# Float64 weights in six staging places, the shifted words in PSUM, token weights in three pieces

## The chip, the cores and the metric

One core of a Trainium2 chip runs the whole program. The metric is the device time in microseconds (us). The kernel before takes 572.88 us, the median of three runs (572.08 to 574.86).

## The reference, cut to what matters

Four sequences (B = 4) of 576 tokens and 512 channels pass three layers:

```python
x = attn(q, k, v)                        # 8 heads of 64; 4 with a local mask, 4 with a strided one
theta = x @ w_theta                      # layer 2
yr = einsum('ts,bsd->btd', w_tok_r, x * cos(theta))
yi = einsum('ts,bsd->btd', w_tok_i, x * sin(theta))
u = x + yr + yi
x = u + maximum(u @ w_ch, 0)
out = moe2(x)                            # layer 3: 4 causal attention experts, top 2 of 4 by a gate
```

The weights `w_theta`, `w_tok_r`, `w_tok_i` and `w_ch` arrive as float64. The kernel turns each element into float32 and then into a pair hi + lo, because a product is computed as three matmuls: hi times hi, hi times lo, lo times hi.

## The kernel before, in words

X[b] (128 partitions, 4 chunks of 128 channels, 576 tokens) holds the activations of sequence b. The work runs in this order of text: layer 1 of sequence 0 (`attn_pair`, four pairs of heads of three groups each, in PSUM pool `ps0`), and between its pairs the loading of `wth`; then for each sequence b `theta` (two halves h of the channels, five tiles of tokens), `sines`, `rotate` (a TensorE transpose of X[b] into the PSUM tile `xn`, a VectorE product with cos and sin, the split into z_hi on ScalarE or VectorE and z_lo on GpSimd), `tokens` (y, nine chunks of three matmuls per output tile) and, one sequence later, `channels`. Layer 1 of sequence b + 1 is woven in by `next_pair`. Layer 3 follows for all sequences. A planner arranges the instructions of each engine's queue from this text and sets the waits. Each queue runs in order.

A float64 weight is loaded by `load64` in chunks. For each chunk SyncE issues a DMA of the raw pairs of words into X[3] (L127), ScalarE makes a float32 from the upper words with a scaled Prelu (L129, into a staging place `st` in X[2]), VectorE shifts and masks it in place (L130), and VectorE ors in the top bits of the lower words, in place again (L131). `split_w` then makes hi on ScalarE (L98) and lo on VectorE (L102 for the scaled `wth`, L100 where c % 3 == 1) or GpSimd (other L100). X[2] and X[3] are free at that time, since layer 1 has not yet reached sequences 2 and 3. Four chunks can be staged at a time. A new DMA waits until L131 has read the place that it overwrites. `wth` takes 8 chunks of 256 columns, `wtk` 18 of 288 (nine before the sines of half 0, nine behind them) and `wch` 8 of 256, 34 in all.

In PSUM each of eight banks holds 512 float32 per partition. `ps0` has four banks for scores, two for transposes and two for the values `av`; `ps1` has two for scores, one for transposes, two for `av`, one for `xn` and two for the accumulators of theta, y and g.

The sines of a half stand behind the last L129 of the `wtk` load before them on ScalarE (`behind`), and the second half of `wtk` stands behind the sines of half 0. `split_act` makes x_hi (L248) and x_lo (L250, GpSimd but for part of the first sequence of layer 3).

Of the kernel before, what the change touches and what calls it, by code (L numbers as in the profile page):

```python
# [24 lines left out]
HALF = S // 2  # L25
# [18 lines left out]
def fused_kernel(ctx: ExitStack, tc: tile.TileContext, ql, kl, vl, qs, ks, vs, wth, wtk, wch, wqk, wvg, wo, out):  # L44
# [71 lines left out]
    def load64(dst, src, kt, n0, n1, scale=1.0):  # L116

        hi, lo = dst
        n = n1 - n0
        for c in range(kt):
            raw = X[3].bitcast(U32)[:, c % 4, :2 * n].rearrange("p (n t) -> p n t", t=2)
            st = X[2][:, c % 4, :n]
            nc.sync.dma_start(raw, src[:, c, n0:n1].bitcast(U32).rearrange("p (n t) -> p n t", t=2))  # L127
            up, low, w = raw[:, :, 1], raw[:, :, 0], st.bitcast(U32)
            got = nc.scalar.activation(st, f(up), AF.Prelu, scale=2.0 ** -112, alpha=2.0 ** 32)  # L129
            nc.vector.tensor_scalar(w, w, 3, 0xFFFFFFF8, op0=ALU.logical_shift_left, op1=ALU.bitwise_and)  # L130
            nc.vector.scalar_tensor_tensor(w, low, 29, w, op0=ALU.logical_shift_right, op1=ALU.bitwise_or)  # L131
            split_w(hi[:, c, n0:n1], lo[:, c, n0:n1], st, scale, nc.vector if c % 3 == 1 else nc.gpsimd)
        return got.ins

    def per_tile(b, pair, g):

        return b == 0 and pair != 2 or b == 1 and g == 0

    ps_of, loaded = {}, {}
# [20 lines left out]
    def attn_pair(b, pair, ps1, apl, deep):  # L160
        ps_of[b] = ps1
# [59 lines left out]
    def values(b, pair, part, xo, turned):  # L221
# [3 lines left out]
        av = ps_of[b].tile([128, 512], F32, tag="av", bufs=2, name=f"av_{b}_{pair}_{r0}")  # L225
# [16 lines left out]
    def split_act(x, name):  # L242
        hi = act.tile([128, S], F32R, tag="ahi", name=f"{name}_hi")
        lo = act.tile([128, S], F32R, tag="alo", name=f"{name}_lo")
        if len(xsplit) == B:
            nc.scalar.copy(hi, x)
        else:
            nc.vector.tensor_copy(hi, x)  # L248
        eng = nc.vector if len(xsplit) == B and name.endswith(("0", "2")) else nc.gpsimd
        eng.tensor_tensor(lo, x, f(hi), op=ALU.subtract)  # L250
        return hi, lo
# [42 lines left out]
    def rotate(b, h):  # L294
        for t in range(NT):
            w, t0, cs = TW[t], 128 * t, trig[h, t]
            xn = ps1.tile([128, 512], F32, tag="xn", bufs=1, name=f"xn_{b}_{h}_{t}")
# [28 lines left out]
    def tokens(b, h):  # L326
        for n in range(2):
            sl = slice(HALF * n, HALF * (n + 1))
            for m in (2 * h, 2 * h + 1):
                c0 = 128 * (m % 2)  # L330
                y = ps1.tile([128, 512], F32, tag="acc", bufs=2, name=f"y_{b}_{m}_{n}")
                for c in range(9):
                    hi, lo = z[h, c]
                    mm3(y[:, :HALF], hi[:, c0:c0 + 128], lo[:, c0:c0 + 128], wtk_hi[:, c, sl], wtk_lo[:, c, sl],
                        c == 0, c == 8)
                u = X[b][:, m, sl]
                nc.vector.tensor_tensor(u, y[:, :HALF], u, op=ALU.add)  # L337
        for n in range(2):
            sl = slice(HALF * n, HALF * (n + 1))
# [28 lines left out]
    with tc.tile_pool(name="ps0", bufs=2, space=PSUM) as ps0, tc.tile_pool(name="ain0", bufs=9) as ain0, \  # L368
            tc.tile_pool(name="apl0", bufs=5) as apl0:
        for pair in range(4):  # L370
            load_pair(0, pair, ain0, 4, 4)
        attn_pair(0, 0, ps0, apl0, 2)
        attn_pair(0, 1, ps0, apl0, 2)
        for n0 in range(0, DM, 256):
            load64(wth_s, wth, 4, n0, n0 + 256, INV2PI)
# [5 lines left out]
    ps1 = ph1.enter_context(tc.tile_pool(name="ps1", bufs=2, space=PSUM))  # L381
    ain = pha.enter_context(tc.tile_pool(name="ain", bufs=3, side="right"))
# [8 lines left out]
    for b in range(B):  # L391
# [4 lines left out]
        else:  # L396
            sines(b, 0, angles, load64(wtk_s, wtk, 9, 0, HALF))
# [7 lines left out]
        else:  # L405
            with tc.issue_after(sins[0, 0]):
                ready = load64(wtk_s, wtk, 9, HALF, S)
# [15 lines left out]
        if b == 0:  # L423
            with tc.issue_after(sins[0, 1]):
                for n0 in range(0, DM, 256):
                    load64(wch_s, wch, 4, n0, n0 + 256)
# [332 lines left out]
```

## Time and profile before

| | |
|---|---|
| median of three runs | 572.88 us |
| profiled execution | 571.9 us, its span 570.1 us |
| TensorE busy | 533.8 us, 94% |
| VectorE busy | 407.2 us, 71% |
| ScalarE busy | 320.3 us, 56% |
| GpSimd busy | 231.1 us, 41% |
| mean granted TensorE clock | 0.97 |

The busy shares are means over stages of a different kind. The first 106 us (layer 1 of sequence 0, all loading of float64 weights, the first thetas and tokens) look different from the rest, and the change touches little outside them; so the profile is read by stretches of time. A row of a stretch gives the busy time of each engine with the count of instructions, then the granted clock, where 1.00 is 2.4 GHz and 0.50 is 1.2 GHz.

### The profile page before, as it was taken

The page shows a single profiled execution, that of the slowest core. Times are in us where ns is not written, and L with a number is a line of the kernel's source. Part 1 is how long each engine was busy: PE and PEld are TensorE (multiplying, and loading weights), DVE is VectorE, ACT ScalarE, POOL GpSimd, SP SyncE. Part 2 cuts the span into 40 slices and gives each one's busy share as a digit, 9 for nine tenths or more (in the row PEclk, how much of TensorE's full clock was granted, in tenths as well). Part 3 has the DMA queues.
Part 4 walks back from the last instruction along what each step waited for, and adds up shares of the span by engine and source line. Part 5 has one row for each costly group of instructions (what it writes and reads, how often), then busy time and mean ns, then how long its engine had stood idle before and what let it go on. Part 6 is the DMA issues. An engine that isn't in the chain of part 4 may idle for free.

```text
span 570.1 us, 12472 instructions
## 1 busy us (share of the span) xinstructions
PE 533.8 (94%) x4504; PEld 508.3 (89%) x4504; DVE 407.2 (71%) x1205; ACT 320.3 (56%) x904; POOL 231.1 (41%) x317
## 2 busy tenths in 40 slices
PE   7859698899999999999999999898999999999986
PEld 6749598899999999999999999897989999999986
DVE  3898889757686556766256553589988898888971
ACT  5875976525435326263152550376778668867873
POOL 3444566421156111545004570354455533634441
PEclk9959689999999999999999999999999999999998
DMA  9659443323122003110100020100001000100012
GB/s 299 208 171 317 126 153 96 97 86 131 31 86 86 23 17 132 37 30 1 56 1 1 1 58 0 39 1 2 0 12 43 33 1 32 54 1 12 33 43 85
DMA packets 19814, 37.55 MB, mean 66 GB/s; under 512 B 2328, under 2 KB 9672, under 8 KB 19752
## 3 DMA queue, kind: packets, MB, share of 16 engines
q1 hardware_dynamic: 19752, 36.74, 20.1%
q8 instruction: 36, 0.59, 0.5%
q14 instruction: 26, 0.21, 0.1%
HBM read 32.01 MB, written 4.72 MB: 64 GB/s over the span
## 4 chain that ended last, share of the span: by engine, by line
PE 60%; DVE 20%; ACT 11%; issue 3%; DMA 3%; POOL 1%; SPq 0%; DVEq 0%; POOLq 0%; ACTq 0%
PE y L254 6%; PE y L255 6%; PE y L256 6%; PE s L179 4%; DVE nm L588 3%; PE th L254 3%; DVE X L131 3%; PE th L256 3%; PE th L255 3%; PE g L255 2%; PE g L254 2%; PE g L256 2%; PE av L232 2%; ACT p L599 2%; PE tp L609 2%
## 5 line engine op out<-in xcount | busy, mean ns | idle before, releaser
L254 PE MATMUL y<-wtk_hi,zhi 128*128 128x288 f32 x288 | 86.5, 301 | 0.5 <-DVE X L337 0.4
L255 PE MATMUL y<-wtk_lo,zhi 128*128 128x288 f32 x288 | 85.9, 299 | 0.0
L256 PE MATMUL y<-wtk_hi,zlo 128*128 128x288 f32 x288 | 84.7, 296 | 0.0
L322 POOL TENSOR_TENSOR zlo<-cs,zhi 128x512 fp32r<-128x512 f32 (+1 forms) x40 | 48.4, 1222 | 66.5 <-DVE zhi L319 45.5
L206 POOL TENSOR_TENSOR p<-p,sm 128x288 f32<-128x288 f32 (+2 forms) x48 | 30.6, 644 | 92.7 <-DVE sm L205 49.0
L606 POOL TENSOR_SCALAR p<-p,sm,gt 128x256 f32<-128x256 f32 (+1 forms) x64 | 45.5, 714 | 51.9 <-DVE sm L604 35.5
L599 ACT ACTIVATE p<-s,nm 128x128 f32<-128x128 f32 (+2 forms) x96 | 49.6, 518 | 15.1 <-DVE nm L588 7.9
L254 PEld LDWEIGHTS y<-wtk_hi,zhi 128*128 128x128 f32 x288 | 54.0, 188 | 1.7 <-DVE X L337 1.1
L250 POOL TENSOR_TENSOR x_lo<-X,x_hi 128x576 fp32r<-128x576 f32 x24 | 35.7, 1492 | 46.9 <-DVE x_hi L248 40.6
L255 PEld LDWEIGHTS y<-wtk_lo,zhi 128*128 128x128 f32 x288 | 54.1, 188 | 0.3
L256 PEld LDWEIGHTS y<-wtk_hi,zlo 128*128 128x128 f32 x288 | 53.9, 188 | 0.1
L254 PE MATMUL th<-wth_hi,x_hi 128*128 128x256 f32 (+1 forms) x160 | 48.5, 303 | 3.3 <-ACT X L239 2.9
L588 DVE TENSOR_REDUCE nm<-s 128x1 f32<-128x128 f32 (+2 forms) x96 | 44.2, 468 | 5.3 <-PE s L586 4.4
L256 PE MATMUL th<-wth_hi,x_lo 128*128 128x256 f32 (+1 forms) x160 | 46.2, 290 | 0.0
L255 PE MATMUL th<-wth_lo,x_hi 128*128 128x256 f32 (+1 forms) x160 | 46.2, 289 | 0.0
L179 PE MATMUL s<-k,q 128*108 128x54 f32 (+2 forms) x320 | 44.0, 283 | 1.7 <-DMA k<-in_kl 1.7
L179 PEld LDWEIGHTS s<-k,q 128*108 128x108 f32 (+1 forms) x320 | 42.1, 204 | 2.7 <-DMA q<-in_ql 1.4
L213 ACT COPY pt<-tp 96x384 f32<-96x384 f32 (+2 forms) x44 | 20.9, 478 | 36.3 <-PE tp L209 36.1
L254 PE MATMUL pq<-x_hi,wqk_hi 128*128 128x288 f32 x128 | 39.8, 311 | 1.0 <-DVE q L534 0.9
L254 PE MATMUL g<-u_hi,wch_hi 128*128 128x288 f32 x128 | 39.2, 306 | 0.0
L618 DVE TENSOR_TENSOR ptlo<-tp,pthi 128x128 fp32r<-128x128 f32 (+4 forms) x80 | 37.6, 478 | 1.2 <-ACT pthi L617 0.6
L255 PE MATMUL pq<-x_lo,wqk_hi 128*128 128x288 f32 x128 | 38.0, 297 | 0.0
(170 smaller groups left out, 1716.3 us busy)
## 6 DMA issues: line engine op xcount, KB each, us to landing
X<-in_wtk SPq DMA_DIRECT2D x18, 288.0 KB
q<-in_qs SPq DMA_DIRECT2D x8, 594.0 KB
q<-in_ql SPq DMA_DIRECT2D x8, 576.0 KB
v<-in_vl SPq DMA_DIRECT2D x24, 144.0 KB
out_t<-X SPq DMA_DIRECT2D x16, 160.0 KB
k<-in_kl SPq DMA_DIRECT2D x8, 304.0 KB
k<-in_ks SPq DMA_DIRECT2D x8, 288.0 KB
X<-in_wth SPq DMA_DIRECT2D x8, 256.0 KB
```

What stands on the lines that cost most here:

```text
L179: nc.tensor.matmul(s[:rm, i * kw:i * kw + w], qt[:, j0 + i, :], kt[:, k0:k0 + w], start=False, stop=i == n - 1)
L206: nc.gpsimd.tensor_tensor(tiles(p), tiles(p), each(sm), op=ALU.mult)
L213: copy(pt[:kw, :n * rm], tp[:kw, :n * rm])
L250: eng.tensor_tensor(lo, x, f(hi), op=ALU.subtract)
L254: nc.tensor.matmul(ps, ahi, bhi, start=first, stop=False)
L255: nc.tensor.matmul(ps, ahi, blo, start=False, stop=False)
L256: nc.tensor.matmul(ps, alo, bhi, start=False, stop=last)
L322: nc.gpsimd.tensor_tensor(lo, zf, f(hi), op=ALU.subtract)
L588: nc.vector.tensor_reduce(nm[:w, t + ci:t + ci + 1], s[:w, :c1 - c0], axis=AX.X, op=ALU.max, negate=True)
L599: nc.scalar.activation(p[:w, c0:c1], scs[ci][:w, :c1 - c0], AF.Exp, bias=nm[:w, t:t + 1], scale=1.0, accum_out=acc)
L606: eng.tensor_scalar(p[:w, :kn], p[:w, :kn], sm[:w, t:t + 1], gt[:w, t, e:e + 1], op0=ALU.mult, op1=ALU.mult)
L618: nc.vector.tensor_tensor(dst(ptlo), src, f(dst(pthi)), op=ALU.subtract)
```

## The change

`load64` gets six staging places of 768 columns, three each in X[2] and X[3]; a place holds 512 words of raw pairs and 256 of `st`. They are used in turn over all loads, so a DMA waits for the chunk six before it. L130 no longer writes in place: it writes the shifted words to a piece `cv` of PSUM, and L131 reads the lower words from SBUF and `cv` from PSUM and writes `st`.

The PSUM for it is found by halving two banks. In `ps0` the two `av` tiles of sequence 0 become halves of one bank, and `cv` gets the two halves of the bank that is free. In `ps1` the `xn` tile becomes one persistent bank `xn_cv`: columns 0 to 255 take the transposes of `rotate`, 256 to 511 are `cv`.

A place holds 256 columns, so `wtk` is loaded in pieces of 256, 160 and 160 tokens, 27 chunks in place of 18. The first piece stands where the first half stood, the other two where the second half stood. `tokens` computes y in 256 and 320 tokens (`QCUT`) in place of 288 and 288, and splits u likewise; `channels` keeps 288 and 288.

Two smaller edits: all four x_lo of the first theta go to VectorE (`not xsplit` holds while the first list is built), and group 1 of the two local pairs of sequence 0 takes the softmax with one exponential for the group and VectorE's subtraction and sum, in place of one exponential with its own sum for each tile (`per_tile`).

```diff
--- before.py
+++ after.py
@@ -113,7 +113,7 @@
     def new_split(pool, kt, n, name):
         return tuple(pool.tile([128, kt, n], F32R, name=f"{name}_{part}") for part in ("hi", "lo"))
-    def load64(dst, src, kt, n0, n1, scale=1.0):
+    def load64(dst, src, kt, n0, n1, cvs, scale=1.0):
@@ -122,21 +122,26 @@
         hi, lo = dst
         n = n1 - n0
         for c in range(kt):
-            raw = X[3].bitcast(U32)[:, c % 4, :2 * n].rearrange("p (n t) -> p n t", t=2)
-            st = X[2][:, c % 4, :n]
+            at = len(staged) % 6
+            staged.append(n0)
+            place = X[2 + at // 3].rearrange("p c s -> p (c s)")[:, 768 * (at % 3):768 * (at % 3) + 768]
+            raw = place[:, :2 * n].bitcast(U32).rearrange("p (n t) -> p n t", t=2)
+            st = place[:, 512:512 + n]
             nc.sync.dma_start(raw, src[:, c, n0:n1].bitcast(U32).rearrange("p (n t) -> p n t", t=2))
             up, low, w = raw[:, :, 1], raw[:, :, 0], st.bitcast(U32)
             got = nc.scalar.activation(st, f(up), AF.Prelu, scale=2.0 ** -112, alpha=2.0 ** 32)
-            nc.vector.tensor_scalar(w, w, 3, 0xFFFFFFF8, op0=ALU.logical_shift_left, op1=ALU.bitwise_and)
-            nc.vector.scalar_tensor_tensor(w, low, 29, w, op0=ALU.logical_shift_right, op1=ALU.bitwise_or)
+            cv = cvs[c % len(cvs)][:, :n].bitcast(U32)
+            nc.vector.tensor_scalar(cv, w, 3, 0xFFFFFFF8, op0=ALU.logical_shift_left, op1=ALU.bitwise_and)
+            nc.vector.scalar_tensor_tensor(w, low, 29, cv, op0=ALU.logical_shift_right, op1=ALU.bitwise_or)
             split_w(hi[:, c, n0:n1], lo[:, c, n0:n1], st, scale, nc.vector if c % 3 == 1 else nc.gpsimd)
         return got.ins
     def per_tile(b, pair, g):
-        return b == 0 and pair != 2 or b == 1 and g == 0
-
-    ps_of, loaded = {}, {}
+        return b == 0 and pair != 2 and (pair > 1 or g != 1) or b == 1 and g == 0
+    loaded, avs, staged = {}, [], []
     def load_pair(b, pair, ain, qbufs, kbufs):
         local = pair < 2
@@ -158,7 +163,6 @@
         loaded[b, pair] = qt, kt, vgs
     def attn_pair(b, pair, ps1, apl, deep):
-        ps_of[b] = ps1
         local = pair < 2
         groups, rw, kw = (LOCAL, LQ, LK) if local else (STRIDED, RQ, RQ)
         qt, kt, loads = loaded[b, pair]
@@ -222,7 +226,11 @@
         local = pair < 2
         rw, kw = (LQ, LK) if local else (RQ, RQ)
         r0 = part[0][0]
-        av = ps_of[b].tile([128, 512], F32, tag="av", bufs=2, name=f"av_{b}_{pair}_{r0}")
+        if b == 0:
+            av = av0[len(avs) % 2]
+            avs.append(av)
+        else:
+            av = ps1.tile([128, 512], F32, tag="av", bufs=2, name=f"av_{b}_{pair}_{r0}")
         with tc.issue_after(turned.ins) if b else nullcontext():
             for j0, pt, wd, vg in part:
                 for i, wi in enumerate(wd):
@@ -246,7 +254,7 @@
             nc.scalar.copy(hi, x)
         else:
             nc.vector.tensor_copy(hi, x)
-        eng = nc.vector if len(xsplit) == B and name.endswith(("0", "2")) else nc.gpsimd
+        eng = nc.vector if not xsplit or len(xsplit) == B and name.endswith(("0", "2")) else nc.gpsimd
         eng.tensor_tensor(lo, x, f(hi), op=ALU.subtract)
         return hi, lo
@@ -294,7 +302,7 @@
     def rotate(b, h):
         for t in range(NT):
             w, t0, cs = TW[t], 128 * t, trig[h, t]
-            xn = ps1.tile([128, 512], F32, tag="xn", bufs=1, name=f"xn_{b}_{h}_{t}")
+            xn = xn_cv[:, :256]
             for c in range(2):
                 nc.tensor.transpose(xn[:w, 128 * c:128 * c + 128], X[b][:, 2 * h + c, t0:t0 + w], ident)
             if t < 4:
@@ -325,18 +333,18 @@
     def tokens(b, h):
         for n in range(2):
-            sl = slice(HALF * n, HALF * (n + 1))
+            sl = slice(*QCUT[n])
             for m in (2 * h, 2 * h + 1):
                 c0 = 128 * (m % 2)
                 y = ps1.tile([128, 512], F32, tag="acc", bufs=2, name=f"y_{b}_{m}_{n}")
                 for c in range(9):
                     hi, lo = z[h, c]
-                    mm3(y[:, :HALF], hi[:, c0:c0 + 128], lo[:, c0:c0 + 128], wtk_hi[:, c, sl], wtk_lo[:, c, sl],
+                    mm3(y[:, :sl.stop - sl.start], hi[:, c0:c0 + 128], lo[:, c0:c0 + 128], wtk_hi[:, c, sl], wtk_lo[:, c, sl],
                         c == 0, c == 8)
                 u = X[b][:, m, sl]
-                nc.vector.tensor_tensor(u, y[:, :HALF], u, op=ALU.add)
+                nc.vector.tensor_tensor(u, y[:, :sl.stop - sl.start], u, op=ALU.add)
         for n in range(2):
-            sl = slice(HALF * n, HALF * (n + 1))
+            sl = slice(*QCUT[n])
             for m in (2 * h, 2 * h + 1):
                 if n == 0:
                     us[m] = (zu.tile([128, S], F32R, tag="zuhi", name=f"u_{b}_{m}_hi"),
@@ -367,18 +375,24 @@
     wch_s = wch_hi, wch_lo = new_split(wb, 4, DM, "wch")
     with tc.tile_pool(name="ps0", bufs=2, space=PSUM) as ps0, tc.tile_pool(name="ain0", bufs=9) as ain0, \
             tc.tile_pool(name="apl0", bufs=5) as apl0:
+        av0, cv0 = ([bank[:, :256], bank[:, 256:]] for bank in (
+            ps0.tile([128, 512], F32, tag=tag, bufs=1, name=tag)
+            for tag in ("av0", "cv0")))
         for pair in range(4):
             load_pair(0, pair, ain0, 4, 4)
         attn_pair(0, 0, ps0, apl0, 2)
         attn_pair(0, 1, ps0, apl0, 2)
         for n0 in range(0, DM, 256):
-            load64(wth_s, wth, 4, n0, n0 + 256, INV2PI)
+            load64(wth_s, wth, 4, n0, n0 + 256, cv0, INV2PI)
         for pair in range(2, 4):
             attn_pair(0, pair, ps0, apl0, 2)
     zu = ph1.enter_context(tc.tile_pool(name="zu", bufs=4))
     rp = ph1.enter_context(tc.tile_pool(name="rp", bufs=5))
     z1 = ph1.enter_context(tc.tile_pool(name="z1", bufs=1))
     ps1 = ph1.enter_context(tc.tile_pool(name="ps1", bufs=2, space=PSUM))
+    xn_cv = ps1.tile([128, 512], F32, tag="xn", bufs=1, name="xn_cv")
+    cv1 = [xn_cv[:, 256:]]
     ain = pha.enter_context(tc.tile_pool(name="ain", bufs=3, side="right"))
     apl = pha.enter_context(tc.tile_pool(name="apl", bufs=3, side="right"))
@@ -394,7 +408,8 @@
             next_pair(b, 0)
             channels(b - 1)
         else:
-            sines(b, 0, angles, load64(wtk_s, wtk, 9, 0, HALF))
+            ready = load64(wtk_s, wtk, 9, 0, 256, cv1)
+            sines(b, 0, angles, ready)
             load_pair(1, 0, ain, 2, 2)
         rotate(b, 0)
         if b > 0:
@@ -404,7 +419,8 @@
             next_pair(b, 2)
         else:
             with tc.issue_after(sins[0, 0]):
-                ready = load64(wtk_s, wtk, 9, HALF, S)
+                for n0 in (256, 416):
+                    ready = load64(wtk_s, wtk, 9, n0, n0 + 160, cv1)
             sines(b, 1, angles, ready)
         rotate(b, 1)
         if b == B - 1:
@@ -423,7 +439,7 @@
         if b == 0:
             with tc.issue_after(sins[0, 1]):
                 for n0 in range(0, DM, 256):
-                    load64(wch_s, wch, 4, n0, n0 + 256)
+                    load64(wch_s, wch, 4, n0, n0 + 256, cv1)
             next_pair(b, 2)
         next_pair(b, 3)
         tokens(b, 1)
```

## Rows read from the trace of the kernel before

**Rows 1.** Stretches: PE, PEld, DVE, ACT, POOL busy (count), granted clock, DMA share, GB/s

```profile
10.00:18.90 8.90, 8.90 (x80) 8.49 (x80) 5.13 (x21) 7.53 (x36) 3.39 (x6) 1.00 0.98 345
18.90:42.20 23.30, 14.03 (x193) 11.68 (x191) 22.29 (x61) 18.42 (x70) 11.35 (x12) 0.70 0.53 160
42.20:61.00 18.80, 17.14 (x131) 16.49 (x131) 15.03 (x37) 12.22 (x34) 6.17 (x7) 0.92 0.75 249
61.00:82.00 21.00, 17.15 (x125) 14.95 (x124) 20.26 (x55) 17.06 (x53) 14.64 (x15) 0.67 0.60 185
82.00:106.00 24.00, 21.35 (x187) 19.60 (x186) 21.38 (x40) 16.17 (x40) 14.86 (x15) 1.00 0.31 96
...
200.00:300.00 100.00, 99.53 (x908) 96.99 (x907) 58.57 (x154) 40.00 (x88) 25.92 (x27) 1.00 0.12 38
```

**Rows 2.** L130 alone by stretches: DVE busy (count), granted clock, DMA share, GB/s

```profile
18.90:61.00 42.10, 8.65 (x17) 0.80 0.63 200
61.00:82.00 21.00, 3.63 (x9) 0.67 0.60 185
82.00:106.00 24.00, 2.73 (x8) 1.00 0.31 96
```

**Rows 3.** L131 alone by the same stretches

```profile
18.90:61.00 42.10, 9.26 (x17) 0.80 0.63 200
61.00:82.00 21.00, 6.09 (x9) 0.67 0.60 185
82.00:106.00 24.00, 7.75 (x8) 1.00 0.31 96
```

**Rows 4.** VectorE lines: count: shortest/median/longest in ns, first and last start

```profile
L130 DVE TENSOR_SCALAR X<-X x34: 250/298/1996, 19.4 to 99.1; 128x288 uint32<-128x288 uint32 x18, 128x256 uint32<-128x256 uint32 x16
L131 DVE SCALAR_TENSOR_TENSOR X<-X,X x34: 405/456/1650, 20.2 to 101.5; 128x288 uint32<-128x288 uint32 x18, 128x256 uint32<-128x256 uint32 x16
L277 DVE TENSOR_SCALAR cs<-th x40: 406/420/425, 48.2 to 313.8; 128x256 f32<-128x256 f32 x32, 64x256 f32<-64x256 f32 x8
L278 DVE SCALAR_TENSOR_TENSOR cs<-cs,th x40: 392/411/422, 48.9 to 315.8; 128x256 f32<-128x256 f32 x32, 64x256 f32<-64x256 f32 x8
L250 DVE TENSOR_TENSOR x_lo<-X,x_hi x8: 748/1366/1582, 313.1 to 490.7; 128x576 fp32r<-128x576 f32 x8
```

**Rows 5.** Timeline of GpSimd and VectorE near 24 us: start, us, engine, line

```profile
23.71 1.41 POOL L250 TENSOR_TENSOR x_lo<-X,x_hi 128x576 fp32r<-128x576 f32 x1
24.02 1.38 DVE L131 SCALAR_TENSOR_TENSOR X<-X,X 128x256 uint32<-128x256 uint32 x1
```

**Rows 6.** Timeline where layer 1 of sequence 0 ends and theta begins

```profile
41.39 0.46 ACT L129 ACTIVATE X<-X 128x288 f32<-128x288 f32 x1 [1.11 <-DMA X<-in_wtk]
41.75 0.39 ACT L239 COPY X<-av 128x144 f32<-128x144 f32 x1
42.19 0.58 PE L254 MATMUL th<-wth_hi,x_hi 128*128 128x256 f32 x1 [2.88 <-ACT X L239]
```

**Rows 7.** A ScalarE group kept apart by shape: count, busy, mean ns, idle before

```profile
L129 ACT ACTIVATE X<-X 128x288 f32<-128x288 f32 x18 | 7.9, 459 | 3.9 <-DMA X<-in_wtk 3.3 <-DVE wtk_lo L100 0.5
```

**Rows 8.** Timeline of VectorE: the first reading of theta of half 1

```profile
68.57 0.41 DVE L277 TENSOR_SCALAR cs<-th 128x256 f32<-128x256 f32 x1
```

**Rows 9.** TensorE groups kept apart by shape: widths 288, 320 and 256

```profile
L256 PE MATMUL y<-wtk_hi,zlo 128*128 128x288 f32 x288 | 84.7, 296 | 0.0
...
L256 PE MATMUL po<-ohi,wo_lo 128*128 128x320 f32 x32 | 9.9, 309 | 0.0
L256 PE MATMUL po<-ohi,wo_lo 128*128 128x256 f32 x32 | 9.3, 290 | 0.0
```

**Rows 10.** Timeline where the last tokens end and the last channels begin

```profile
343.39 0.29 PE L256 MATMUL y<-wtk_hi,zlo 128*128 128x288 f32 x1
343.52 0.29 PE L254 MATMUL g<-u_hi,wch_hi 128*128 128x288 f32 x1
...
344.68 0.46 DVE L347 TENSOR_TENSOR u_lo<-X,u_hi 128x288 fp32r<-128x288 f32 x1 [0.50 <-ACT u_hi L346]
```

## The prediction, made before the change was run

> **What bounds the kernel now.** I read the slices of the page first (which stretches keep TensorE full), then busy time by stretches, then the lines of VectorE inside the stretches that are not full, last the timeline at the joints. From about 106 us on TensorE is the bound: it is busy 99.53 of 100 us between 200 and 300 [rows 1]. An edit there pays only through TensorE's own work, and this change leaves that alone. Before 106 us it is otherwise. VectorE is busy 22.29 of 23.30 us in the first stretch with float64 work, 20.26 of 21.00 in the third and 21.38 of 24.00 in the fourth, while TensorE is busy 14.03, 17.15 and 21.35, in the first and third at a mean granted clock of 0.70 and 0.67, so partly at 1.2 GHz [rows 1]. TensorE's idle time from 18.9 to 106 us is 9.27 + 1.66 + 3.85 + 2.65 = 17.4 us, and more is lost at the low clock. What is saved on VectorE's path here comes back at the end nearly one for one, since a full TensorE follows. 17.4 us bounds the gain from idle time.
>
> Why is VectorE so busy? L131 takes 405 ns at its shortest and 1650 at its longest, L130 250 and 1996, while L277 and L278, which have an operand in PSUM, stay within 406 to 425 and 392 to 422 ns in all 40 executions [rows 4]. The timeline shows what stretches them: an L131 that begins 0.31 us into GpSimd's x_lo ends within 0.3 us of its end, 1.38 us long [rows 5]. So a VectorE instruction with its operands in SBUF may have to sit out a GpSimd instruction, and one fed from PSUM never did here.
>
> **The change part by part.** *Shifted words in PSUM.* L131 becomes the form of L278 (one source in SBUF, one in PSUM), 0.41 us for 256 columns. L130 (SBUF to PSUM) has no row. Its ends are 0.25 us, its own shortest in SBUF, and 0.42 us, L277, which crosses the other way. I take 0.42, as crossing to PSUM is what L277 shares with it [rows 4]. In the first two stretches (18.9 to 61 us) 17 chunks took 8.65 + 9.26 = 17.9 us [rows 2, 3]; 17 × 0.83 = 14.1, a gain of 3.8 us. In the fourth, 8 chunks took 2.73 + 7.75 = 10.5 us and will take 6.6, a gain of 3.8.
>
> The Trainium skill, "SBUF — State Buffer", section "Who interferes with whom", says that VectorE contends with GpSimd when it has two SBUF inputs or runs in a two-port mode, and not with one SBUF input outside those modes. By that rule both new forms are free of waits, and the rows above agree for L277 and L278; the sum is the same with or without it.
>
> *Three pieces.* In the third stretch nine chunks of 288 columns become 18 of 160. VectorE paid 3.63 + 6.09 = 9.7 us for them [rows 2, 3]. An instruction of 160 columns costs between 0.26 us (the 0.41 in proportion) and 0.41 us (no shorter); I take 0.32, about the middle: 18 × 0.64 = 11.5 us, 1.8 us more (ends 9.4 and 14.8). ScalarE pays more: L129 takes 0.459 us at 288 columns [rows 7], and I price L98, its partner over the same columns, alike, so nine pairs took 8.3 us; at 0.35 each (ends 0.25 in proportion and 0.46) 18 pairs take 12.6, 4.3 us more, and its 17.06 busy us become 21.4 in a stretch of 21 [rows 1]. ScalarE so becomes as tight as VectorE there. SyncE issues nine more DMAs; it mostly waits for places anyway, so I cost them at nothing. Should the next sequence's q and k queue behind them, TensorE would wait for keys.
>
> *Six places.* A DMA is issued two chunks sooner. At the joint to theta, ScalarE's L129 waited 1.11 us for its DMA, with the last copy of layer 1 queued behind it and theta waiting for that copy [rows 6]. I take these 1.1 us as gained (ends 0 and 2).
>
> *x_lo on VectorE.* Four instructions of at least 0.75 us (their median elsewhere is 1.37) [rows 4] put 3.0 us onto a full VectorE. They take four of 1.41 us off GpSimd [rows 5], each of which had stretched something on VectorE; what L130 and L131 lost is in the sum above, and I give back 1.3 us for lo instructions stretched in the same way (ends 0 and 2).
>
> *Softmax of two groups.* It adds two passes per group on VectorE and removes short ones on ScalarE. This lies between 10 and 18.9 us, where VectorE has 3.8 us free and ScalarE is at 7.53 of 8.90 [rows 1]. I cost it at 0. Without that cover four passes of about 0.4 us would cost 1.6.
>
> *One bank for the values.* With two banks the values of a second group need not wait for anyone to empty the first. With both halves in one bank, I expect them to wait for ScalarE's copy of the first, a copy of 0.39 us and its place in the queue [rows 6]. At the last pair this is on the path: 1.0 us (ends 0 and 2).
>
> *xn and cv in one bank.* The order of text now holds: chunks of pieces 2 and 3 come after the whole `rotate` of half 0, and the transposes of half 1 after all chunks. The first half of this helps. Theta of half 1 is read first at 68.57 us [rows 8], behind rotation products and chunks mixed on VectorE; with the rotation first I take it 3 us earlier (ends 0 and 6).
>
> *y in 256 and 320.* Same columns, same number of matmuls: 290 and 309 ns on another line average 299.5 against 296 [rows 9], 0 to 3 us over 864 matmuls; I take 0, since these durations overlap. Where layer 2 ends, `channels` at 288 columns now needs the second u, too. There u_lo ends at 345.14 us, 1.6 us after the first g matmul starts. Nine matmuls of three other chunks, at the 0.13 us between two starts, cover 1.2 us; it costs 0.4 us (ends 0 and 1.6) [rows 10]. Before, the other half of y was the cover.
>
> Sum to 61 us: −3.8 + 3.0 − 1.3 − 1.1 + 1.0 = −2.2. Third stretch: +1.8 − 3 = −1.2. Fourth: VectorE saves 3.8, but TensorE idles only 2.65 us there; I take half of the latter, −1.3, the rest shows other waits. End: +0.4. Together −4.3 us; with shorter idle less of the first and third stretch runs at 1.2 GHz, for which I add −1. So −5.3: 571.9 becomes 566.6 for the profiled execution, and on the median of 572.88 it is **567.6**.
>
> **The rivals.** *The idle time mostly goes:* order and waits both fall into place, and TensorE gets back some 12 of the 17.4 idle us: 561. For it: all stretched instructions sit on a full VectorE. Against it: ScalarE's added load.
>
> *No change:* what VectorE gains goes to x_lo (3.0) and the third stretch (1.8), and theta still starts behind the values' copies: −2.2 + 1.8 = −0.4 without the 3 us, 572.5.
>
> *Slower, by the shared bank:* transposes of half 1 must wait for the last of 18 chunks, and chunks for the last transpose of half 0. If ScalarE paces the chunks, 18 pairs and its other work take the 21.4 us only after the rotation (some 3 us after the sines), so the last chunk is ready about 3.4 us later than now, and y's second piece, rotation and everything behind follow. With 1.6 for the joint at the end and 0.4 of the other terms unreturned, the change is +4 to +6: 578. It decides once TensorE has no other matmuls for that time; half of y now needs the first piece alone, 54 matmuls, which speaks against it. The Trainium skill, "PSUM — Partial Sum Buffer", section "PSUM bank collisions raise a hardware error", gives the reason for such waits: engines must be kept apart by bank, not by address. No row of before shows the price.
>
> **How the numbers follow.** Forecast (564 to 570) 0.42, idle time mostly goes (under 564) 0.20, no change 0.20, slower 0.18. Half a per cent, 2.9 us, is about what a measurement of this kernel can tell. Faster by more than that 0.62, within it 0.20, slower 0.18. The range 559 to 577 leaves out the far ends of the first and last case, about 2 in 10; the forecast's own is 564 to 570.
>
> **What would show it.** L130 and L131 near 0.42 and 0.41 us with no long ones; VectorE's L250 near 0.75; theta starting about 2 us before 42.19; its half 1 read near 65; y starting before 80 us; TensorE idle before 106 us down by some 4 us. It is wrong if ScalarE is full from 61 to 85 us and y waits for the last piece, or if xn waits for `cv`.

## The result: slower, 579.0 us in place of 573.8

The kernel after takes 578.98 us (median of 4 runs, 578.33 to 580.85), the kernel before 573.77 beside it (572.08 to 574.86): a ratio of 1.011, 95% interval 1.0084 to 1.0135. The forecast was 567.6. The profiled execution of after took 579.21 us with a span of 577.4, 7.3 us longer than before's 570.1, at a clock of 0.967 (before 0.97). After's line numbers are higher (old → new): L127 → L130, L129 → L132, L130 → L135, L131 → L136, L206 → L210, L239 → L247, L248 → L256, L250 → L258, L254–L256 → L262–L264, L321 → L329, L322 → L330, L337 → L345; L98, L100 and L102 stay. In kernels with a line added ahead of them all are one higher still. Some executions of the kernels below were disturbed and far slower (g2's profiled one took 868.23 us); the ratios leave them out, the medians do not.

Busy time of after by stretch, the columns as in [rows 1]:

```profile
18.90:42.20 23.30, 16.43 (x207) 13.43 (x203) 17.21 (x55) 16.86 (x66) 4.84 (x8) 0.68 0.45 135
61.00:82.00 21.00, 17.01 (x148) 15.00 (x148) 15.70 (x48) 17.04 (x52) 11.04 (x15) 0.76 0.41 117
82.00:106.00 24.00, 20.67 (x156) 19.59 (x153) 16.07 (x51) 18.13 (x53) 9.58 (x14) 0.86 0.58 182
200.00:300.00 100.00, 99.89 (x936) 97.15 (x936) 60.33 (x154) 36.81 (x80) 26.46 (x27) 1.00 0.14 43
```

VectorE went from 22.29 to 17.21 us in the first of these and from 21.38 to 16.07 in the third: it is not full there any more. These falls are not all savings, since work moved out of the stretches: only 8 conversions start in the first (before 14), and those of `wch`, which lay in the third, follow behind 106 us, up to 132. Over the whole load L130 and L131 took 38.1 us for 34 chunks, L135 and L136 take 32.2 for 43. TensorE's idle time from 18.9 to 106 us fell from 17.4 to 15.5 us, but y starts at 82.3 us (before 80.6). The conversions alone, by tile (shortest, median, longest, in ns), between 18.9 and 106 us:

```profile
L135 DVE TENSOR_SCALAR xn_cv<-X x27: 309/328/428, 44.7 to 97.1; 128x160 uint32<-128x160 uint32 x18, 128x256 uint32<-128x256 uint32 x9
L135 DVE TENSOR_SCALAR cv<-X x8: 410/418/428, 21.4 to 32.5; 128x256 uint32<-128x256 uint32 x8
L136 DVE SCALAR_TENSOR_TENSOR X<-X,xn_cv x27: 284/320/420, 45.7 to 97.4; 128x160 uint32<-128x160 uint32 x18, 128x256 uint32<-128x256 uint32 x9
L136 DVE SCALAR_TENSOR_TENSOR X<-X,cv x8: 405/412/422, 22.1 to 34.2; 128x256 uint32<-128x256 uint32 x8
```

No instruction is stretched, and the prices are those of the forecast. But the first row also says that the first conversion of `wtk` (tile `xn_cv`) starts at 44.7 us; before, it started at 33.1. VectorE's timeline at that place (start, us, instruction, and in brackets the idle time ahead of it with what ended it):

```profile
34.50 0.74 DVE L258 TENSOR_TENSOR x_lo<-X,x_hi 128x576 fp32r<-128x576 f32 x1
37.38 0.42 DVE L102 SCALAR_TENSOR_TENSOR wth_lo<-X,wth_hi 128x256 fp32r<-128x256 f32 x1 [2.14 <-ACT wth_hi L98]
39.48 0.46 DVE L256 CAST x_hi<-X 128x576 fp32r<-128x576 f32 x1 [1.67 <-ACT X L247]
39.97 0.76 DVE L258 TENSOR_TENSOR x_lo<-X,x_hi 128x576 fp32r<-128x576 f32 x1
44.28 0.46 DVE L256 CAST x_hi<-X 128x576 fp32r<-128x576 f32 x1 [3.56 <-ACT X L247]
44.66 0.42 DVE L135 TENSOR_SCALAR xn_cv<-X 128x256 uint32<-128x256 uint32 x1
```

VectorE idles for 7.4 of these 10 us, while ScalarE has prepared the first chunks of `wtk` since 32.7. The conversion starts when ScalarE's last copy of layer 1 (L247) is done and theta starts. The chunks behind it are late, too: the first of piece 2 is shifted at 75.4 us, of before's second half at 61.7. The waits of the first 125 us show it (engine and line, what it waited for: us in total, times, longest; the last row is before's, where TensorE waited for no `wtk_hi`):

```profile
POOL wtk_lo L100 <- ACT wtk_hi L98: 36.4, 13, 13.7
ACT X L132 <- DMA X<-in_wtk: 10.0, 11, 2.5
PE y L262 <- ACT wtk_hi L98: 3.3, 3, 2.6
...
POOL wtk_lo L100 <- ACT wtk_hi L98: 3.9, 4, 1.2
```

The second loss lies far from the changed load, in the last tokens of layer 2. GpSimd's timeline there, and TensorE's:

```profile
335.41 1.28 POOL L330 TENSOR_TENSOR zlo<-cs,zhi 128x512 fp32r<-128x512 f32 x1 [3.09 <-ACT zhi L329]
337.45 3.77 POOL L100 TENSOR_TENSOR wqk_lo<-wqk_st,wqk_hi 128x512 fp32r<-128x512 f32 x3 [0.76 <-ACT wqk_hi L98]
341.17 0.72 POOL L330 TENSOR_TENSOR zlo<-cs,zhi 128x256 fp32r<-128x256 f32 x1
...
341.95 0.50 PE L264 MATMUL y<-wtk_hi,zlo 128*128 128x256 f32 x2 [1.36 <-POOL zlo L330]
342.86 0.41 PE L262 MATMUL y<-wtk_hi,zhi 128*128 128x320 f32 x1 [0.40 <-DVE X L345]
```

Three `wqk_lo` of layer 3 stand ahead of the last `zlo`, and TensorE waits for it. Before, two stood there, and TensorE did not wait:

```profile
331.65 2.55 POOL L100 TENSOR_TENSOR wqk_lo<-wqk_st,wqk_hi 128x512 fp32r<-128x512 f32 x2 [0.75 <-ACT wqk_hi L98]
334.15 0.95 POOL L322 TENSOR_TENSOR zlo<-cs,zhi 128x256 fp32r<-128x256 f32 x1
```

### The profile page after: what moved, and what is told of

The parts are those of the page before. It is cut to its first block, busy times and chain, and to the rows that moved or that the text cites. A ratio compares the mean times of both kernels' runs of the same rounds, so it can differ in the third digit from the quotient of the medians.

```text
span 577.4 us, 12544 instructions
## 1 busy us (share of the span) xinstructions
PE 538.8 (93%) x4504; PEld 512.4 (89%) x4504; DVE 401.0 (69%) x1234; ACT 319.9 (55%) x910; POOL 222.0 (38%) x319
## 4 chain that ended last, share of the span: by engine, by line
PE 59%; DVE 17%; ACT 13%; DMA 4%; issue 4%; POOL 2%; SPq 0%; ACTq 0%; POOLq 0%; DVEq 0%
PE y L262 6%; PE y L264 5%; PE y L263 5%; PE s L183 4%; PE av L240 3%; PE g L262 3%; PE th L262 3%; DVE nm L604 3%; PE g L264 3%; PE g L263 3%; PE th L263 2%; PE th L264 2%; DMA X<-in_wtk 2%; PE tp L625 2%; ACT p L615 2%
## 5 line engine op out<-in xcount | busy, mean ns | idle before, releaser
L262 PE MATMUL y<-wtk_hi,zhi 128*128 128x320 f32 (+1 forms) x288 | 87.4, 307 | 3.7 <-ACT wtk_hi L98 3.3
L264 PE MATMUL y<-wtk_hi,zlo 128*128 128x320 f32 (+1 forms) x288 | 86.1, 302 | 1.5 <-POOL zlo L330 1.5
L263 PE MATMUL y<-wtk_lo,zhi 128*128 128x320 f32 (+1 forms) x288 | 86.4, 302 | 0.0
L330 POOL TENSOR_TENSOR zlo<-cs,zhi 128x512 fp32r<-128x512 f32 (+1 forms) x40 | 47.2, 1191 | 63.4 <-DVE zhi L327 41.6
L210 POOL TENSOR_TENSOR p<-p,sm 128x288 f32<-128x288 f32 (+2 forms) x48 | 29.5, 622 | 86.1 <-DVE sm L209 68.6
L262 PEld LDWEIGHTS y<-wtk_hi,zhi 128*128 128x128 f32 x288 | 55.0, 192 | 5.0 <-ACT wtk_hi L98 4.0
L264 PEld LDWEIGHTS y<-wtk_hi,zlo 128*128 128x128 f32 x288 | 54.8, 192 | 2.2 <-POOL zlo L330 1.9
L262 PE MATMUL th<-wth_hi,x_hi 128*128 128x256 f32 (+1 forms) x160 | 48.4, 303 | 2.4 <-DVE cs L286 1.7
L604 DVE TENSOR_REDUCE nm<-s 128x1 f32<-128x128 f32 (+2 forms) x96 | 44.3, 469 | 5.3 <-PE s L602 4.4
L183 PE MATMUL s<-k,q 128*108 128x54 f32 (+2 forms) x320 | 44.7, 283 | 2.0 <-DMA k<-in_kl 1.9
L264 PE MATMUL th<-wth_hi,x_lo 128*128 128x256 f32 (+1 forms) x160 | 46.0, 289 | 0.0
L258 POOL TENSOR_TENSOR x_lo<-X,x_hi 128x576 fp32r<-128x576 f32 x20 | 29.9, 1496 | 34.6 <-DVE x_hi L256 23.4
L262 PE MATMUL pq<-x_hi,wqk_hi 128*128 128x288 f32 x128 | 39.8, 311 | 1.0 <-DVE q L550 0.7
L262 PE MATMUL g<-u_hi,wch_hi 128*128 128x288 f32 x128 | 38.9, 305 | 1.7 <-DVE X L367 1.7
## 6 DMA issues: line engine op xcount, KB each, us to landing
v<-in_vl SPq DMA_DIRECT2D x24, 144.0 KB
```

The costliest lines, as they stand in the source:

```text
L183: nc.tensor.matmul(s[:rm, i * kw:i * kw + w], qt[:, j0 + i, :], kt[:, k0:k0 + w], start=False, stop=i == n - 1)
L210: nc.gpsimd.tensor_tensor(tiles(p), tiles(p), each(sm), op=ALU.mult)
L262: nc.tensor.matmul(ps, ahi, bhi, start=first, stop=False)
L263: nc.tensor.matmul(ps, ahi, blo, start=False, stop=False)
L264: nc.tensor.matmul(ps, alo, bhi, start=False, stop=last)
L330: nc.gpsimd.tensor_tensor(lo, zf, f(hi), op=ALU.subtract)
```

## The experiments

Four theories were tried. Theory 1: the place in PSUM holds the `wtk` load back, at the hand-over of the bank from layer 1 to layer 2 or by its order with `rotate`. Theory 2: the three pieces. Theory 3: the halved `av` bank. Theory 4, formed after the first four runs: the cut of y changes GpSimd's queue at the end. All ratios are to the kernel before. Beside them three times are read from TensorE's timeline of each profiled execution: the start of the first theta, the time from there to the first y of sequence 1, and the time from the first y of sequence 3 to the end of the last g. One execution was profiled of each kernel; those of e3 and e7 are the longest of theirs (585.12 and 577.08 us). The recorded expectations count the layers from 0, so their layers 0 and 1 are layers 1 and 2 here; y7 is the y of sequence 3's half 1.

| run | median us | ratio (95%) | first theta | from there to y of sequence 1 | y of sequence 3 to end of last g |
|---|---|---|---|---|---|
| before | | | 42.2 | 129.7 | 43.1 |
| after | 578.98 | 1.0110 (1.0084–1.0135) | 44.3 | 133.0 | 45.8 |
| e1 | 581.53 | 1.0129 (1.0086–1.0173) | 48.2 | 129.0 | 45.8 |
| e3 | 580.88 | 1.0139 (1.0080–1.0197) | 48.5 | 128.9 | 45.8 |
| e5 | 578.05 | 1.0075 (1.0034–1.0116) | 43.9 | 124.6 | 47.4 |
| e6 | 579.34 | 1.0100 (1.0065–1.0135) | 42.0 | 127.7 | 47.4 |
| e8 | 583.68 | 1.0147 (1.0074–1.0220) | 45.0 | 132.1 | 47.4 |
| g1 | 574.43 | 1.0029 (1.0005–1.0053) | 41.5 | 132.4 | 43.2 |
| g4 | 569.66 | 0.9944 (0.9921–0.9968) | 43.5 | 125.3 | 43.1 |
| h2 | 574.68 | 1.0031 (1.0013–1.0048) | 41.5 | 133.1 | 43.1 |
| h3 | 575.06 | 1.0044 (1.0027–1.0060) | 42.0 | 133.1 | 44.1 |
| h5 | 569.38 | 0.9940 (0.9914–0.9966) | 42.1 | 125.1 | 43.1 |
| e7 | 571.44 | 0.9984 (0.9956–1.0012) | 45.5 | 129.4 | 43.1 |

Of the 7.3 us by which after's profiled span is longer, 2.1 lie ahead of the first theta, 3.3 between it and sequence 1's y and 2.8 in the last column; the rest gives the difference back.

**All shifts in place (e1), and the load's new shape put into the kernel before (e3).** In e1 all calls give `None` for `cvs`, and L135 writes to its own place again; e3 has before's lines for the shifts, with these from after:

```diff
-            cv = cvs[c % len(cvs)][:, :n].bitcast(U32)
+            cv = cvs[c % len(cvs)][:, :n].bitcast(U32) if cvs else w
```

```diff
+            at = len(staged) % 6
...
-                ready = load64(wtk_s, wtk, 9, HALF, S)
+                for n0 in (256, 416):
+                    ready = load64(wtk_s, wtk, 9, n0, n0 + 160)
...
-            sl = slice(HALF * n, HALF * (n + 1))
+            sl = slice(*QCUT[n])
```

> The kernel after, with all shifted words back in place in the raw pieces' staging in SBUF; the six places, the three pieces of wtk, the y cut, the halved av bank and x_lo on VectorE stay. Theory 1 (the place in PSUM gates the load: layer 1's first conversion waits for the bank that layer 0 gives up, and the later ones stand in one order with rotate's tiles): without it the first wtk conversion starts near 33 us again instead of 44.7, the second channel half's rotate starts before 90 instead of 101, and the time is 572 to 575 us, because the long L130 and L131 of before come back as well. Theory 2 (three pieces instead of two: 18 smaller chunks more on ScalarE and SP): the load still ends near 97 to 100 us, the time stays 577 to 580. Theory 3 (the halved av bank): theta still starts 2 us late, 44 to 44.5, and at least 2 of the 5.2 us stay: 576 or more.

> The kernel before, with the six places for raw pieces, the three pieces of wtk and the y cut of 256 and 320 tokens; shifts in place in SBUF, av in two banks, x_lo on GpSimd. Theory 1 (the PSUM place is the cause): 570 to 574.5 us, theta starts at 42.2, the second y piece isn't held by wtk_hi for more than 1 us. Theory 2 (the three pieces are the cause): 576 to 579 us, y waits for wtk_hi from L98 by 2 us or more, as in the kernel after.

Theory 1 as it stood fell: nothing came back. (In e3 TensorE's y waits for no `wtk_hi`, as theory 1 had it, but the time and theta are not theory 1's.) In e1 theta now started at 48 us, for a reason that no theory had. GpSimd, TensorE and VectorE in e1's timeline:

```profile
29.96 5.01 POOL L210 TENSOR_TENSOR p<-p,sm 108x216 f32<-108x216 f32 x1 [3.63 <-ACT p L200]
...
35.02 0.92 PE L213 MATMUL tp<-ident,p 108*54 108x108 f32 x4 [4.72 <-POOL p L210]
...
29.71 0.38 DVE L102 SCALAR_TENSOR_TENSOR wth_lo<-X,wth_hi 128x256 fp32r<-128x256 f32 x1
...
33.81 0.74 DVE L258 TENSOR_TENSOR x_lo<-X,x_hi 128x576 fp32r<-128x576 f32 x1
```

At other places of this trace instructions of this shape take 0.54 to 0.91 us. Here it lasts until 0.4 us after VectorE's run of gapless instructions ends (34.55). Between the two VectorE rows lie 16 more instructions, all in SBUF but for two short reads of PSUM (L208). So in place the load seems to keep GpSimd out of the softmax for that long; in after, with PSUM, the same instruction takes 0.55 to 0.61 us. That also means that e1 took away a gain together with the suspected loss; single pieces had to be tried.

**Piece 1 alone in place (e5); pieces 2 and 3 alone (e6).** With e1's line for `cv`, the one call in e5 and the other in e6:

```diff
-            ready = load64(wtk_s, wtk, 9, 0, 256, cv1)
+            ready = load64(wtk_s, wtk, 9, 0, 256, None)
...
-                    ready = load64(wtk_s, wtk, 9, n0, n0 + 160, cv1)
+                    ready = load64(wtk_s, wtk, 9, n0, n0 + 160, None)
```

> The kernel after, with the first piece of wtk (256 tokens) shifted in place in SBUF, the two others and wch in PSUM. Theory 1 holds two gates: the hand-over of the bank from layer 0 to layer 1 (first conversion at 44.7 us) and the one order with rotate (second piece from 75.4). This takes only the first away: first wtk conversion near 33 to 36 us, but the second piece's first conversion still at 73 to 76 and the table load for the sines of half 1 still at 92 us or later; 577 to 579.5 us. If the hand-over alone were the cause: 573 to 575. Theory 2 (number of pieces): 577 to 580 and the load's end unmoved even where its conversions are free.

> The kernel after, with the second and third pieces of wtk (160 tokens each) shifted in place in SBUF, the first piece and wch in PSUM. Theory 1 with the order behind rotate as the larger gate: the second piece's conversions start before 70 us instead of 75.4, the table load for the sines of half 1 comes at 80 to 88 instead of 94.7, rotate of half 1 starts before 92 instead of 101; 573 to 575.5 us. If the hand-over at 44.7 were the larger gate: the load is late all the same, 577 to 579. Theory 2 (three pieces on ScalarE): 577 to 580, ScalarE over 90% busy from 61 to 82.

The medians hardly moved, but the profiles did: sequence 1's y came 124.6 and 127.7 us after theta instead of 133.0. The start's loss was gone or smaller, and another had stayed hidden behind it. (e5's time fits theory 1, but its pieces did not start where theory 1 had them: 30.5 and 69.3 us, not 33 to 36 and 73 to 76.) e6 says one thing more. It still waits for the bank: its first `wtk` conversion starts at 42.30, 0.35 us behind theta. With pieces 2 and 3 in place that late start alone does not, in this one trace, cost what it costs in after; it takes the shared bank for them as well. All five kernels so far with the cut for every sequence need 45.8 to 47.4 us for the last column's stretch, before needs 43.1. In e5 TensorE's clock fell there, behind a wait of 1.38 us for `zlo`, and once more 30 us on (windows of 10, 10 and 30 us; the clock is the last column but two, and e6's fell in the same places):

```profile
330.00:340.00 10.00, 8.05 (x52) 7.44 (x50) 3.35 (x7) 4.56 (x11) 8.16 (x8) 0.89 0.25 71
340.00:350.00 10.00, 9.88 (x66) 9.65 (x65) 2.31 (x5) 1.71 (x4) 1.49 (x2) 0.94 0.03 10
370.00:400.00 30.00, 26.98 (x180) 25.26 (x180) 25.51 (x89) 19.35 (x56) 14.48 (x23) 0.89 0.00 1
```

That is why the last column of e5, e6 and (below) e8 is 1.5 us longer than after's 45.8. Two more stretches eat what e5 and e6 gained. From sequence 1's y to sequence 3's they take 144.1 and 144.0 us, after 141.2; no run says why. Behind the last g they take 2.8 and 2.7 us more than after, where the clock fell.

**The cut (g2, g1, h2) and GpSimd's queue (h3).** g2 is the kernel before with the cut alone, g1 is after with it for sequence 0 only (`b < B - 1` in place of `b == 0` makes h2):

```diff
-            sl = slice(HALF * n, HALF * (n + 1))
+            sl = slice(*QCUT[n])
...
-            sl = slice(*QCUT[n])
+            sl = slice(*(QCUT if b == 0 else HCUT)[n])
```

> The kernel before with one edit: y and u in 256 and 320 tokens in place of 288 and 288; two pieces of wtk, four places, everything else as before. Theory 4 (new, from the four runs so far: in all five kernels with this cut the last tokens, y7, take 17.5 to 19.1 us instead of 15.4, because the planner then puts three wqk_lo of L100 instead of two in front of the last zlo on GpSimd's queue, and TensorE waits for that zlo): the start is as before (theta at 42.2, y0 at 80.6, th6 at 285 within 1.5 us), y7 takes 17.5 us or more, layer 2 ends 2 to 4 us later, 575 to 577.5 us. Theory 2 (the three pieces of wtk) and theory 1 (the place in PSUM) both say 572.5 to 573.5, no change, since neither is in this kernel.

> The kernel after, with the cut of 256 and 320 for sequence 0 alone; sequences 1 to 3 take y and u in 288 and 288 again. Theory 4: GpSimd's queue has two wqk_lo ahead of the last zlo again, y7 takes 15.2 to 15.8 us instead of 17.5, and 2 to 4 us come back: 575 to 577 us; what is left over 572.8 belongs to the start. Theories 1 and 2: the end of layer 2 keeps its delay, 578 to 580.

g2: 1.0080 (1.0043 to 1.0117), slower by the cut alone. Of its profiled execution only the order is used: there, too, three `wqk_lo` stand ahead of the last `zlo`. g1 has two again and got 4.5 us back. h2 has the halves in sequence 3 alone, h3 keeps the cut everywhere and only moves the last `zlo` ahead:

```diff
-            nc.gpsimd.tensor_tensor(lo, zf, f(hi), op=ALU.subtract)
+            lows[b, h] = nc.gpsimd.tensor_tensor(lo, zf, f(hi), op=ALU.subtract).ins
...
-                with tc.issue_after(turns[b, 1]):
+                with tc.issue_after(turns[b, 1]), tc.issue_after(lows[b, 1]):
                     wqk_hi, wqk_lo = load_split(wc, ws, wqk, 4, 512, "wqk")
```

> The kernel after, with the cut of 256 and 320 for sequences 0 to 2 and 288 and 288 for sequence 3 alone. Theory 4 places the whole loss of the cut at the last tokens: y7 15.2 to 15.9 us, 573.5 to 576, as the run with the cut for sequence 0 alone (574.4). If the cut costs in every sequence: a third of the 4.5 us comes back, 577 to 578.

> The kernel after, with one edit: the lo halves of wqk and wvg (L100) are queued on GpSimd behind the last zlo (L330) of sequence 3, so that none of them stands ahead of it; the cut of 256 and 320 stays for all sequences. Theory 4, with GpSimd's order as its mechanism: the last zlo ends about 3.8 us sooner against the zlo before it (three of 1.26 us gone), TensorE has no wait of over 0.4 us for it, y7 takes 15.2 to 15.9 us instead of 17.5, and the time falls to 574 to 576.5. If the end's loss lies in the cut itself (u in two unequal pieces in front of the channels' matmuls, or the wider matmuls), y7 or g3 stay long: 578 to 580.

Both came out as theory 4 said, 574.68 and 575.06. GpSimd's timeline in h3:

```profile
333.23 1.28 POOL L330 TENSOR_TENSOR zlo<-cs,zhi 128x512 fp32r<-128x512 f32 x1 [3.09 <-ACT zhi L329]
335.21 0.74 POOL L330 TENSOR_TENSOR zlo<-cs,zhi 128x256 fp32r<-128x256 f32 x1 [0.69 <-DVE zhi L327]
335.91 3.78 POOL L100 TENSOR_TENSOR wqk_lo<-wqk_st,wqk_hi 128x512 fp32r<-128x512 f32 x3
```

All that TensorE waited for from 331 to 349 us in h3:

```profile
PE y L262 <- DVE X L345: 0.3, 1, 0.3
PE y L264 <- POOL zlo L330: 0.2, 1, 0.2
```

So by the medians 3.9 us of the cut's 4.5 (578.98 − 575.06, 578.98 − 574.43) are the order on GpSimd; the intervals leave 1 to 1.5 us either way. The traces place 1.8 of them in the last column (45.8 in after, 44.1 in h3), and 1.5 more in an execution whose clock falls there as in e5; what after's own four executions lost beyond the 1.8 is not shown. The last column of h3, 44.1 against 43.2 in g1, leaves 0.9 us for the cut itself.

**What of the shifted words belongs into PSUM (e8, g4, h5).** e8 shifts only `wth` there (`cv1 = None`, with e1's line for `cv`). g4 is e5 with the cut for sequence 0 alone. h5 is g1 with the bank taken from a pool that outlasts both layers:

```diff
+    psx = ph1.enter_context(tc.tile_pool(name="psx", bufs=1, space=PSUM))
+    xn_cv = psx.tile([128, 512], F32, name="xn_cv")
...
-        av0, cv0 = ([bank[:, :256], bank[:, 256:]] for bank in (
-            ps0.tile([128, 512], F32, tag=tag, bufs=1, name=tag)
-            for tag in ("av0", "cv0")))
+        bank = ps0.tile([128, 512], F32, tag="av0", bufs=1, name="av0")
+        av0, cv0 = ([t[:, :256], t[:, 256:]] for t in (bank, xn_cv))
...
-    xn_cv = ps1.tile([128, 512], F32, tag="xn", bufs=1, name="xn_cv")
```

> The kernel after, with the shifted words of wth alone in PSUM; wtk and wch are shifted in place in SBUF. Six places, three pieces, the cut for all sequences stay. Theory 1 for the start (either gate of the PSUM place in layer 1's pool costs what e1, with long waits between VectorE and GpSimd at theta, could not show): theta starts at 42 to 44.5 as in the kernel after and not at 48 as with all in place, y2 starts at 168 to 172 instead of 177.3; with theory 4's end left in, 575.5 to 578 us. Theory 2 (three pieces): y2 at 176 or later, 578 to 581.

> The run with the first piece of wtk in place (e5) once more, with the cut of 256 and 320 for sequence 0 alone. In e5 all of sequence 1 to 3 up to y6 stood 0.6 to 1.3 us ahead of the kernel before, and only y7 and what follows were late. If theory 4 holds for the end and theory 1's hand-over for the start, both losses are gone: y7 15.2 to 15.8 us, 571 to 573.5 us, level with the kernel before or a little faster. If the start's loss has another cause: 575 to 577.

> The kernel after with the cut for sequence 0 alone, and the bank of xn and cv taken from a pool that lasts over both layers: wth's shifted words use both of its halves, so layer 1's pool has to wait for no bank of layer 0 before the first wtk conversion. All shifted words stay in PSUM. Theory 1 with the hand-over as the gate: first wtk conversion at 33 to 36 us instead of 44.7, y2 starts 124 to 128 us after theta (132.3 in the run with the cut for sequence 0 alone, 125.3 where the first piece was shifted in place as well), 568.5 to 571.5 us. If the gate is the order with rotate in the shared bank, or the PSUM place for the first piece itself: y2 131 or more after theta, 573.5 to 575.5.

e8 came out where theory 2 had y of sequence 1 (177.1 us; the ratio of 1.0147 rests on three executions of 576 to 584 us), not theory 1, though its first `wtk` conversion starts at 32.0 us. With all of `wtk` and `wch` in place VectorE is full again:

```profile
82.00:106.00 24.00, 20.48 (x184) 19.35 (x182) 23.71 (x53) 18.16 (x53) 15.37 (x17) 1.00 0.45 140
```

h5 came out as theories 1 and 4 said, g4 a little faster, with the same three pieces, so theory 2 falls: three pieces alone do not cost this. The times of e1, e3 and e8, a little above those of theory 2, go with stretched conversions: L135 and L136, or their lines there, take 35.9, 40.0 and 39.1 us in all (32.2 in after, 32.3 in h5). How much of each time that is was not separated. In h5 all words are shifted in PSUM, and the order of chunks behind `rotate` is that of after; only the hand-over is gone. VectorE's first `wtk` conversion (L136 here, then its L137), ScalarE's `wtk_hi` right behind it, and theta's start:

```profile
32.62 0.41 DVE L136 TENSOR_SCALAR xn_cv<-X 128x256 uint32<-128x256 uint32 x1
...
33.78 0.41 DVE L137 SCALAR_TENSOR_TENSOR X<-X,xn_cv 128x256 uint32<-128x256 uint32 x1
...
34.22 0.42 ACT L99 ACTIVATE wtk_hi<-X 128x256 fp32r<-128x256 f32 x1
...
42.14 0.58 PE L263 MATMUL th<-wth_hi,x_hi 128*128 128x256 f32 x1 [0.51 <-ACT X L248]
```

All that TensorE waited for from 77 to 106 us, where after had 3.3 us of it:

```profile
PE y L263 <- ACT wtk_hi L99: 0.7, 1, 0.7
```

The conversion starts 9.5 us ahead of theta instead of 0.4 behind it. g1 to h5, 574.43 to 569.38, prices the hand-over at 5.1 us in a kernel whose three pieces all use the shared bank (e6 has the hand-over without that). h5 and g4 are also faster than the kernel before, by 0.6%.

**The two small edits (e7)**, alone in the kernel before:

```diff
-        return b == 0 and pair != 2 or b == 1 and g == 0
+        return b == 0 and pair != 2 and (pair > 1 or g != 1) or b == 1 and g == 0
...
-        eng = nc.vector if len(xsplit) == B and name.endswith(("0", "2")) else nc.gpsimd
+        eng = nc.vector if not xsplit or len(xsplit) == B and name.endswith(("0", "2")) else nc.gpsimd
```

> The kernel before with the two smaller edits alone: the four x_lo of the first theta on VectorE, and group 1 of the two local pairs of sequence 0 with one exponential for the group. The prediction costs them at +3.0 - 1.3 and 0 us on VectorE's path to theta: 573 to 575. If taking x_lo off GpSimd frees more waits of VectorE than it adds: 571 to 572.5. Neither theory 1 nor theory 4 is touched; a time over 576 would say that a part of the loss lies here.

571.44 us, 1.3 below before; the interval, −2.5 to +0.7 us, leaves out the +1.7 of the prediction, and does not tell a gain from none.

## Why the prediction was wrong, step by step

*What bounds the kernel*, and *shifted words in PSUM*: right. L135 takes 0.42 and L136 0.41 us, none is long, and together they take 32.2 us, as the prediction's three parts add up (14.1 + 11.5 + 6.6). With both losses out of the way the change gains: h5 stands 3.4 us below before (572.75 beside it; 1.9 to 4.9 by the interval), where the sum said 5.3. TensorE's idle time from 18.9 to 106 us is 13.5 us in h5, down by the 4 that were forecast. What is gained does not all come back at the end: h5 is 4.7 us ahead of before at sequence 1's y and 3.5 at sequence 3's. Of the Trainium skill, "SBUF — State Buffer", section "Who interferes with whom", the rule that an instruction with one SBUF input doesn't contend outside the two-port modes held in all 70 of after's conversion instructions above (the longest took 0.428 us).

*xn and cv in one bank* is the first step that failed. It priced the order of chunks and `rotate` at −3 and never asked from whom the bank comes. The tile `xn_cv` is taken from layer 2's pool, whose banks are layer 1's until the last values are copied out, so the load's start moved from 9 us ahead of theta to 0.4 behind it. Half 1 of theta was read at 70.84 us, not earlier than before's 68.57 [rows 8]; without the hand-over, in h5, it was read at 66.92, so 1.7 of the 3 us are there. Measured: +5.1 for a wait that the sum did not have, in place of −3; e6's trace says that it costs this much only while pieces 2 and 3 use the bank, too. Whether the wait itself or the planner's place for it, behind the last cast of x_hi, holds the conversion, the trace doesn't tell; the lasting bank removes both.

*y in 256 and 320* is the second. It was costed by its matmuls (0) and by the u at the end (+0.4; measured 0.9 for the two). That the planner may arrange a queue anew when sizes change was not in it. The cut of y put a third `wqk_lo` ahead of a `zlo`: +3.9 us. The working stood in that very place [rows 10], but GpSimd's queue there was not read.

*Three pieces*: L135 and L136 at 160 columns take 0.32 us each, 0.64 as forecast. ScalarE was not full from 61 to 82 us (17.04 instead of 21.4), as only 6 of the 18 chunks lie there. g4 and h5 have these pieces and are the fastest. One of the prediction's signs of being wrong came true in part: y did wait for `wtk_hi`, 3.3 us in after, but not for a full ScalarE; in h5 it is 0.7.

*Six places*: nothing gained at the joint; an L132 there still waits 1.59 us for its DMA (before 1.11 [rows 6]).

*One bank for the values*: the wait is there. TensorE's values wait for ScalarE's copies six times in after (4.1 us in all in g1, 5.9 in h5), in before for `pt` (the third row) and for no copy:

```profile
PE av L240 <- ACT X L247: 3.7, 4, 1.9
PE av L240 <- ACT X L245: 1.7, 2, 1.5
...
PE av L232 <- ACT pt L213: 3.9, 2, 2.2
```

after starts theta 2.1 us later than before, but this can't be put down to the bank. g1, h2 and h3 have the same instructions in the same order in all queues up to there, and start it at 41.5, 41.5 and 42.0. After's profiled execution was late before any `av`: a set of six score matmuls waits 1.03 us for its keys and starts at 10.46 us, in g1 0.39 us and 9.50. Against 1.0 predicted, no net cost is to be seen at theta; theory 3 got no run of its own, so what two full banks would give stays open. The sum up to theta, −2.2, can't be seen either: g1, h2, h3 and h5 start it at 41.5 to 42.1, before at 42.2.

*x_lo on VectorE and softmax*: L258 takes 0.75 us on the mean there, the 3.0 of the sum; e7's interval says that the two edits together gave back more than the 1.3 of the sum. Which of the two did is not shown.

*The rivals.* The slower one named the shared bank and 578 us, close to the result by luck: its mechanism is another, transposes waiting for chunks. That order is in h5 as well, and there it costs nothing that can be seen. The Trainium skill's "PSUM — Partial Sum Buffer", section "PSUM bank collisions raise a hardware error", with its rule to keep engines apart by bank, stood beside it; no run here shows a price of that rule.

## What to carry to other kernels

When a tile moves to another memory or pool, ask first who holds that place until when, and read the moved instruction's new start against its old one. A change of sizes can re-plan queues far from the edit, so compare the order around each late wait before pricing the edit itself. Busy time by stretch falls when work leaves the stretch, too: count the instructions. Two losses can hide one another: e5 and e6 took one away, and their medians stayed at 578.05 and 579.34.

## What the runs showed of the hardware that was not expected

Beside a VectorE working without a gap on SBUF a 0.55 us GpSimd instruction lasted 5.01 us (e1), while VectorE did 17 of its own. That VectorE held it is read from the times. In e7, which also has x_lo on VectorE and the shifts in place, GpSimd instructions of the same shape took 2.85 us, to 0.34 us behind the end of such a run, and 3.73 us, ending inside one. In after and the other kernels that shift `wth` in PSUM they took 0.55 to 0.61. The rows of before showed only the opposite, VectorE sitting out one instruction of GpSimd [rows 5]. The Trainium skill, "SBUF — State Buffer", section "Who interferes with whom", lets the first one to issue keep the shared ports for the whole of its instruction; here the wait outlasted many.

Executions of the same queues start theta up to 2.8 us apart (41.5 to 44.3). A shift of that size in the first 45 us of one profile is no finding; distances from theta are steadier (132.4 to 133.1 in after, g1, h2 and h3, which have the same order in all queues up to theta).
